# Attention with a window and block summaries, then a two-layer MLP: the first key load leads SyncE's queue, the first unit's probabilities are scaled while TensorE turns them, its means go by transfer, weights get a fourth staging place, and the order table is another

## The chip, the cores and the metric

The kernel runs on one core of a Trainium2 chip. The metric is the device time of a run in microseconds (us), lower is better. TensorE (PE) multiplies matrices, VectorE (DVE), ScalarE (ACT) and GpSimd (POOL) work on elements, SyncE (SP) issues nearly all transfers between the chip's memory (HBM) and the on-chip buffers.

## The reference

q, k and v are float32 with B=4, H=8, S=768, D=64; w_in is 512x2048 and w_out 2048x512, both with 64-bit elements in HBM. Cut to what is computed:

```python
k_sum = k.reshape(B, H, 24, 32, D).max(axis=3)
v_sum = v.reshape(B, H, 24, 32, D).mean(axis=3)
local = scale * q @ k.T          # kept where |pos_q - pos_k| < 16, else -1e9
blocks = scale * q @ k_sum.T + log(32)
a = softmax(concat([local, blocks], axis=-1))
attn = a @ concat([v, v_sum], axis=2)
x = attn.transpose(0, 2, 1, 3).reshape(3072, 512)
h = x @ w_in
out = (h - tanh(h)) @ w_out      # 3072x512, float32
```

## The kernel before, in words

**Units and pairs.** The 3072 rows of x are worked on in eight units of 384 rows (u = 0 to 7, two for each batch). A unit has four pairs of heads (p = 0 to 3). For a pair, TensorE turns keys and queries (`prep`), makes the scores (`scores`, into the PSUM tiles pS and pY), VectorE and ScalarE make the softmax (`softmax`, tile prob), the probabilities are turned (`transpose_probs`, tile probT) and multiplied by the values (`values`, tile vw, into pX or pY), and the result is split into a rounded part xh and a rest xl or vsum (`x_split`), so that products of parts have float32's precision. With the four pairs of a unit, the MLP runs over 16 slices f of w_in and w_out (`moe_in`, `moe_act_small`, `moe_split`, `moe_out`). For units 4 to 7 two units share products (`moe_pair`), and their x is kept in xf and other buffers. TensorE's work on all that is some 5,100 products.

**Softmax in unit 0.** For each of the six tiles of a pair (three row blocks of 128, two heads) VectorE makes mask and maximum and ScalarE an exponential with its sum; for each row block VectorE then makes the two sums and their inverses (stats<-stats), 12 times in the unit. Then `normal` scales the probabilities, 128x118 at a time, 24 times in the unit, on VectorE or ScalarE. `transpose_probs` turns them on TensorE by transposes against the identity. Unit 1 does the same; from unit 2 on, VectorE and transfers turn them.

**Means.** The first values (tile xh, 128x4x384) are halved by an addition (the task "pair", on VectorE or GpSimd), summed by TensorE against a block matrix (pX<-xh,vacc), read out by ScalarE (mean<-pX) and put behind the values of each of the six places in vw (24 rows). Unit 0 does that by four copies (`put_mean`, vw<-mean), the later ones by a transfer.

**Weights.** `convert(i)` (i even: slice i//2 of w_in, odd: of w_out) loads 128x512 elements of 64 bits into one of three staging places (tile raw, RAWB places), and makes float32 of them by four operations (a scaling tmp<-raw, a shift, the sign, a join), then a rounded part and a rest; the whole ones stay in tile wf for unit 0. A place is free again when the join has read it.

**Order.** What runs when is not decided at run time: `ORDER` is a table of task numbers, in which every engine takes its tasks, and `ELSEWHERE` says which engine takes a task that several could. `Plan.follow` goes through it with modelled costs, and where it foresees that TensorE would stand still before 100 us of its own clock, it puts in idle products of the identity with itself, pX<-ident (`keep_warm`); each shows as two records of 128x128. SyncE issues its transfers strictly in the table's order, with 8 in flight at most. Each engine waits by semaphores for what it reads. All instructions are issued through the helper class `Engine`, so every one has the same line, L233 (L235 after the change); the tiles tell them apart.

**End.** The last unit's y is copied out of PSUM by ScalarE (prob<-pS, prob<-pX, prob<-pT) and stored. A second program, for large h, follows behind a branch and is not taken.

Of the kernel before, what the change touches and what calls it, by code (L numbers as in the profile page):

```python
# [29 lines left out]
RAWB = 3  # L30
# [18 lines left out]
def phase(t):  # L49
# [486 lines left out]
def program(  # L536
# [210 lines left out]

    vd = v.rearrange("b h s d -> b s h d")


    def convert(i):
        f = i // 2
        tmp, res, place = ("wt", i), ("w", i), i % RAWB
# [826 lines left out]
```

## Time and profile before

| | |
|---|---|
| median of 3 runs | 641.96 us (640.52 to 648.61) |
| profiled execution | 641.7 us, its span 640.0 us |
| TensorE busy in the span | 624.0 us |
| VectorE, ScalarE, GpSimd busy | 486.6, 422.6, 172.5 us |
| granted clock of TensorE, mean | 0.995 |

The span goes from the first instruction to the end of the last; the time of a run has 1.7 us around it. A share of busy time is an average over the whole program. The views by stretch, the waits with what ended them, and the timelines of single engines tell in which part something can be gained or lost. "[1.41 <-DMA xl<-in_k_dram]" behind a row means that the engine had stood idle for 1.41 us and that this transfer released it.

### The profile page before, as it was taken

What the parts mean: (1) busy time and instruction counts of PE and PEld (TensorE: products, weight loads), DVE (VectorE), ACT (ScalarE), POOL (GpSimd) and SP (SyncE); (2) the same over time, 40 slices, a digit from 0 to 9 for tenths busy, and PEclk for the clock granted to TensorE, in tenths of its full rate; (3) what the DMA queues carried; (4) which work ended last, traced back from release to release, by engine and by line L of the source; (5) the groups of instructions that cost most, each with busy time, mean ns of one, the idle gap of its engine ahead of it and who ended that gap; (6) DMA issues with size and microseconds to landing.
All of it is one profiled execution on the core that took longest, in us unless ns stands there. A gap on an engine that the chain in (4) does not pass through costs nothing.

```text
span 640.0 us, 14660 instructions
## 1 busy us (share of the span) xinstructions
PE 624.0 (97%) x5163; PEld 532.0 (83%) x5163; DVE 486.6 (76%) x1349; ACT 422.6 (66%) x1270; POOL 172.5 (27%) x191
## 2 busy tenths in 40 slices
PE   6989999999999999999999999999999999999996
PEld 5877666688888888888888889988898889989995
DVE  3989999998797787567785788685659878677662
ACT  3979788678767777656767556555557754554545
POOL 2130003134313331130313104235351043315330
PEclk9989999999999999999999999999999999999998
DMA  8867886856687787877875641000000100000002
GB/s 297 199 197 225 226 231 191 182 116 185 162 165 161 186 228 167 186 174 160 236 198 165 192 132 55 0 2 1 0 2 1 65 35 1 1 1 1 2 0 102
DMA packets 159765, 77.27 MB, mean 121 GB/s; under 512 B 121704, under 2 KB 148552, under 8 KB 159688
## 3 DMA queue, kind: packets, MB, share of 16 engines
q1 hardware_dynamic: 159416, 76.09, 46.0%
q8 instruction: 42, 0.69, 0.5%
q14 instruction: 35, 0.29, 0.1%
q10 hardware_dynamic: 272, 0.20, 0.1%
HBM read 58.12 MB, written 17.84 MB: 119 GB/s over the span
## 4 chain that ended last, share of the span: by engine, by line
PE 85%; DVE 6%; DMA 4%; ACT 2%; SPq 1%; issue 1%; POOL 1%; DVEq 0%; POOLq 0%; ACTq 0%
PE pH L233 37%; PE pY L233 30%; PE pS L233 6%; PE pT L233 6%; PE pX L233 6%; DVE raw L233 2%; DMA raw<-in_moe_w_out_dram 1%; DVE tmp L233 1%; DVE prob L233 1%; SPq L233 1%; DMA xl<-in_k_dram 1%; DMA tmp<-in_v_dram 1%; DMA raw<-in_moe_w_in_dram 1%; DVE wf L233 1%; POOL xf L233 1%
## 5 line engine op out<-in xcount | busy, mean ns | idle before, releaser
L233 PE MATMUL pH<-xh,w 128*128 128x384 f32 x608 | 155.9, 346 | 0.0
L233 PE MATMUL pY<-wf,gh 128*128 128x512 f32 x321 | 133.9, 454 | 0.2 <-DVE gh L233 0.2
L233 ACT ACTIVATE prob<-prob,stats 128x118 f32<-128x118 f32 x298 | 109.4, 385 | 35.3 <-DVE stats L233 33.7
L233 PEld LDWEIGHTS pH<-xh,w 128*128 128x128 f32 x608 | 109.0, 188 | 9.2 <-issue 3.1
L233 POOL TENSOR_TENSOR gl<-gu,gh 128x384 fp32r<-128x384 f32 x45 | 46.9, 1041 | 134.1 <-ACT gh L233 71.7
L233 POOL TENSOR_TENSOR gu<-gu,gt 128x384 f32<-128x384 f32 x49 | 51.3, 1048 | 105.8 <-ACT gu L233 60.5
L233 PEld LDWEIGHTS pY<-wf,gh 128*128 128x128 f32 x321 | 59.4, 188 | 19.4 <-issue 10.8
L233 ACT ACTIVATE gu<-gu 128x384 f32<-128x384 f32 x128 | 65.7, 517 | 1.1
L233 ACT ACTIVATE gh<-gu 128x384 fp32r<-128x384 f32 x71 | 36.8, 520 | 42.3 <-PE pY L233 16.7
L233 PE MATMUL pH<-xl,w 128*128 128x384 f32 x192 | 64.6, 336 | 0.0
L233 ACT ACTIVATE gu<-tmp 128x384 f32<-128x384 f32 x64 | 33.2, 518 | 37.2 <-DVE gl L233 19.4
L233 DVE TENSOR_TENSOR gl<-gu,gh 128x384 fp32r<-128x384 f32 x67 | 41.1, 613 | 13.0 <-ACT gh L233 9.3
L233 DVE TENSOR_TENSOR gu<-gu,gt 128x384 f32<-128x384 f32 x63 | 35.5, 567 | 8.7 <-ACT gu L233 8.5
L233 ACT ACTIVATE gt<-pH 128x384 f32<-128x384 f32 x64 | 30.7, 482 | 15.8 <-PE pH L233 15.6
L233 ACT ACTIVATE gu<-pH 128x384 f32<-128x384 f32 x64 | 30.9, 482 | 14.3 <-PE pH L233 9.4
L233 ACT ACTIVATE gt<-tmp 128x384 f32<-128x384 f32 x64 | 32.4, 512 | 11.9 <-DVE tmp L233 7.9
L233 ACT ACTIVATION_READ_ACCUMULATOR prob<-prob,stats 128x1 f32 x192 | 36.6, 190 | 0.0
L233 PE MATMUL pY<-kT,gh 128*128 128x512 f32 x90 | 36.5, 406 | 0.0
L233 PEld LDWEIGHTS pH<-xl,w 128*128 128x128 f32 x192 | 36.0, 187 | 0.0
L233 PE MATMUL pY<-kT,gl 128*128 128x512 f32 x90 | 35.4, 394 | 0.0
L233 POOL TENSOR_TENSOR xf<-xf 128x256 f32<-128x256 f32 x25 | 19.5, 781 | 56.1 <-DVE xf L233 55.0
L233 DVE CUSTOM_DVE_ANT_0 prob<-pS,mask 128x118 f32<-128x118 f32 x96 | 25.6, 275 | 11.6 <-PE pT L233 10.2
(306 smaller groups left out, 1627.9 us busy)
## 6 DMA issues: line engine op xcount, KB each, us to landing
place<-turned SPq DMA_DIRECT2D x96, 96.0 KB
probT<-place SPq DMA_DIRECT2D x24, 384.0 KB
raw<-in_moe_w_in_dram SPq DMA_DIRECT2D x16, 512.0 KB
raw<-in_moe_w_out_dram SPq DMA_DIRECT2D x16, 512.0 KB
vw<-in_v_dram SPq DMA_DIRECT2D x80, 96.0 KB
rawq<-in_q_dram SPq DMA_DIRECT2D x96, 48.0 KB
tmp<-in_v_dram SPq DMA_DIRECT2D x24, 192.0 KB
raw<-in_k_dram SPq DMA_DIRECT2D x48, 96.0 KB
```

The lines of the kernel that those rows point to most:

```text
L233: return lambda *args, **kwargs: self._tc.keep_in_program_order(op(*args, **kwargs))
```

## The change

In unit 0 the inverse sums no longer scale the probabilities. They scale an identity (`diag`: `eye` times two inverse sums, 128x2x64, on VectorE, into the buffer of tile turned), and TensorE's turn is a plain product with that scaled identity where it was a transpose. `eye` is made once on GpSimd. The mean copies of unit 0 are gone; the transfer that the other units use takes their place. All loads of keys, queries, values and weights on SyncE are ordered behind the first key load. Weights get a fourth staging place in the buffer of xf, until units 4 and 5 need that for their x. The sums over chunks of values are trees of additions instead of reductions. The last slice (f = 15) of units 6 and 7 is worked on in three pieces of 128 columns, and one output copy is halved between ScalarE and VectorE. Three numbers of the planner's model are others, and ORDER and ELSEWHERE are other tables from end to end.

```diff
@@ the order, two of some 330 lines of tables
-    2, 6, 0, 1, 332, 9, 10, 7, 8, 13, 24, 220, 222, 224, 221, 226, 223, 252, 225, 254, 28, 35, 3, 14, 255, 227, 228, 230, 234, 232, 40, 258, 238, 236,
...
@@ planner
-    LARGE, TURN = 1.25, 0.9
+    LARGE, TURN = 9.0, 0.9
...
-        moved = nbytes / rate * (1.2 if kind == "w load" else 1.0)
+        moved = nbytes / rate * (1.12 if kind == "w load" else 1.0)
@@ program
+        first_home("xf", "xf", [P, 2 * DM + 64], U32)
+        eye = made["xf"][:, 2 * DM:].bitcast(F32)
...
+    do("const", POOL, 0.3, lambda: gpsimd.tensor_tensor(eye, ident[:, :64], ident[:, 64:], op=ALU.add), r=[IDENT], w=[EYE])
...
+    first_home(("dg",), "turned", [P, 2, 2 * NT, 64])
@@ convert
+    places = RAWB + small_only
...
-        tmp, res, place = ("wt", i), ("w", i), i % RAWB
+        tmp, res, place = ("wt", i), ("w", i), i % places
...
-            return raw[:, 2 * DM * place:2 * DM * (place + 1)]
+            return raw[:, 2 * DM * place:2 * DM * (place + 1)] if place < RAWB else made["xf"][:, :2 * DM]
@@ sum_chunks
-                vector.tensor_reduce(m[:, 1], x.rearrange("r t d -> r d t"), axis=AX.X, op=ALU.add)
+                x, m = at(st)[:96], at(acc)[:96]
+                for n in (4, 2, 1):
+                    to = m[:, 1] if n == 1 else x[:, :n * D]
+                    vector.tensor_tensor(to, x[:, :n * D], x[:, n * D:2 * n * D], op=ALU.add)
@@ put_mean
-        if u < 1:
-            for half in range(2):
-                either("mean copy", {DVE: 0.61, ACT: 0.86}, ...
-            return
@@ softmax
+            if u < 1:
+                i = x[0]
...
+                do("diag", DVE, 0.2, lambda i=i: vector.tensor_tensor(at(("dg", p))[:, 2 * i:2 * i + 2], eye.unsqueeze(1).broadcast_to([P, 2, 64]), at(st)[:, 3 * T + 2 * i:3 * T + 2 * i + 2].unsqueeze(2).broadcast_to([P, 2, 64]), op=ALU.mult), r=[EYE, (st, ("z", i))], w=[(("dg", p), i)])
+                continue
             for i in x:
                 for a in range(2):
                     either("normal", {DVE: 0.19, ACT: 0.3}, ...
@@ transpose_probs
-                        tensor.transpose(to[:, n, a], at(pr)[rows, n, a, :N2], ident[rows, rows])
+                        if u < 1:
+                            tensor.matmul(to[:, n, a], at(pr)[rows, n, a, :N2], at(("dg", p))[rows, 2 * n + a], start=True, stop=True)
+                        else:
+                            tensor.transpose(to[:, n, a], at(pr)[rows, n, a, :N2], ident[rows, rows])
@@ moe_act_small (as in moe_split and in moe_pair's last sum)
-        do("tanh", ACT, 0.37, lambda: scalar.activation(at(t), x(), AF.Tanh, scale=EC), r=[key], w=[(t, 0)])
+        for i, s in cuts(u, f):
+            n, c = seen_at(u, f, i), (s.stop - s.start - U) / 1400
+            do("tanh", ACT, 0.37 + c, lambda s=s: scalar.activation(at(t)[:, s], x()[:, s], AF.Tanh, scale=EC), r=[(key, i)], w=[(t, i)])
...
@@ store_y
+        if PAIRS and (u, i) == (PAIRED[2], NT - 1):
+            h = DM // 2
+            do("y out", ACT, 0.32, lambda: copy(scalar, at(ys)[:, :h], at(y)[:, :h], scale), r=[(y, 0)], w=[key])
+            do("y out", DVE, 0.33, lambda: copy(vector, at(ys)[:, h:], at(y)[:, h:], scale), r=[(y, 0)], w=[(ys, "half")])
...
@@ end of program
+    first = next(t for t in plan.tasks if t.kind == "k load")
+    for t in plan.tasks:
+        if t.kind in ("k load", "v load", "q load", "w load") and SP in t.costs and t is not first:
+            t.order.add(first)
```

The new functions are `cuts(u, f)`, three slices of 128 columns for the last slice of units 6 and 7 and one slice of 384 otherwise, and `seen_at`, the place of such a piece's sum.

SyncE's queue at the program's start. xl takes keys, xh values, rawq queries, vw values for the products, raw weights. Before:

```order
L233 DMA vw_125<-in_v_dram 16x4x64
L233 DMA rawq_96<-in_q_dram 128x2x192
L233 DMA xl<-in_k_dram 128x2x384 x2
L233 DMA xh<-in_v_dram 128x4x384 x2
L233 DMA raw<-in_moe_w_in_dram 128x4x256
L233 DMA raw<-in_moe_w_out_dram 128x1024
```

And now:

```order
L235 DMA xl<-in_k_dram 128x2x384
L235 DMA vw_131<-in_v_dram 16x4x64
L235 DMA rawq_97<-in_q_dram 128x2x192
L235 DMA xl<-in_k_dram 128x2x384
L235 DMA xh<-in_v_dram 128x4x384
L235 DMA raw<-in_moe_w_in_dram 128x4x256
L235 DMA xh<-in_v_dram 128x4x384
L235 DMA raw<-in_moe_w_in_dram 128x4x256
```

One key load stands ahead of the small value load and the query load, and a weight load stands ahead of the second values.

SyncE's queue some ten transfers later, around the first unit's values (vw). Before:

```order
L233 DMA vw_98<-in_v_dram 96x4x64 x4
L233 DMA rawq_271<-in_q_dram 128x2x192
L233 DMA raw<-in_moe_w_in_dram 128x4x256
L233 DMA xl<-in_k_dram 128x2x384
L233 DMA raw<-in_moe_w_out_dram 128x1024
```

And now:

```order
L235 DMA vw_99<-in_v_dram 96x4x64 x3
L235 DMA vw_99<-mean 24x6x256
L235 DMA vw_99<-in_v_dram 96x4x64
L235 DMA raw<-in_moe_w_in_dram 128x4x256
L235 DMA xl<-in_k_dram 128x2x384
L235 DMA vw_131<-in_v_dram 96x4x64
```

The transfer of the mean stands between the value loads, ahead of a weight load and the last key load.

TensorE from the second pair's scores to the turn of the first pair's probabilities (into pT and pY). Before:

```order
L233 MATMUL pS<-kT,q 64x94 x2
L233 MATMUL pY_282<-kT,q 64x94 x2
L233 MATMUL pX<-ident 128x128 x17
L233 MATMUL pT<-ident,prob 118x64
L233 MATMUL pY_368<-ident,prob 118x64
```

And now:

```order
L235 MATMUL pS<-kT,q 64x94 x2
L235 MATMUL pY_283<-kT,q 64x94 x2
L235 MATMUL pX<-ident 128x128 x9
L235 MATMUL pT<-turned,prob 118x64
L235 MATMUL pY_331<-turned,prob 118x64
```

Nine idle products stand where there were 17, and the turn reads turned, the scaled identity, instead of ident; in the whole first stretch they are 23 where there were 37.

## Rows read from the trace of the kernel before

**Rows 1.** The page's busy times: engine, us, share of the span, instructions.
```profile
PE 624.0 (97%) x5163; PEld 532.0 (83%) x5163; DVE 486.6 (76%) x1349; ACT 422.6 (66%) x1270; POOL 172.5 (27%) x191
```

**Rows 2.** Windows: us; busy (instructions) of PE, PEld, DVE, ACT, POOL; clock, DMA, GB/s.
```profile
46.40:128.00 81.60, 81.30 (x612) 55.70 (x611) 76.42 (x195) 67.72 (x180) 9.90 (x9) 1.00 0.80 212
13.00:42.00 29.00, 25.65 (x404) 21.08 (x405) 26.86 (x126) 24.81 (x83) 8.35 (x6) 0.95 0.85 221
40.00:44.00 4.00, 2.85 (x40) 2.38 (x39) 2.69 (x9) 2.66 (x5) 0.00 (x0) 0.67 0.75 225
```

**Rows 3.** Groups, TensorE to 46.4 us: busy us, mean ns, idle before, its releasers.
```profile
L233 PE MATMUL pX<-ident 128*128 128x128 f32 x74 | 12.3, 308 | 5.1 <-POOL ident L233 2.3 <-DVE vsum L233 1.5 <-ACT mean L233 1.2
```

**Rows 4.** Timeline of TensorE: start us, duration us, work, idle before it.
```profile
6.63 0.36 PE L233 MATMUL pH<-ident,xl 64*128 64x64 f32 x1 [1.41 <-DMA xl<-in_k_dram]
...
12.90 1.48 PE L233 MATMUL pX<-xh,vacc 128*24 128x256 f32 x6
...
16.23 0.24 PE L233 MATMUL pS<-top,q 64*64 64x24 f32 x2
...
17.23 4.06 PE L233 MATMUL pX<-ident 128*128 128x128 f32 x34
...
21.22 0.27 PE L233 MATMUL pT<-ident,prob 64*118 64x64 f32 x1
...
21.71 0.87 PE L233 MATMUL pH<-ident,rawq 128*128 128x128 f32 x6
...
24.01 0.92 PE L233 MATMUL pX<-probT,vw 118*64 118x64 f32 x24
...
37.72 0.24 PE L233 MATMUL pT<-ident,prob 64*118 64x64 f32 x1 [1.63 <-DVE prob L233]
```

**Rows 5.** Timelines of VectorE and GpSimd in the first 46 us.
```profile
10.32 0.96 DVE L233 TENSOR_TENSOR xh<-xh 128x768 f32<-128x768 f32 x1 [0.62 <-DMA xh<-in_v_dram]
...
12.45 1.81 POOL L233 TENSOR_TENSOR xh<-xh 128x768 f32<-128x768 f32 x1 [8.56 <-DMA xh<-in_v_dram]
...
17.36 0.07 DVE L233 MEMSET pS<- 64x15 f32 x1 [0.78 <-PE pY L233]
...
45.81 0.56 DVE L233 TENSOR_TENSOR vsum<-pY,xh 128x384 fp32r<-128x384 f32 x1 [0.73 <-ACT xh L233]
```

**Rows 6.** Tile mean: durations in ns (least/median/most), first and last start in us.
```profile
L233 DVE COPY vw<-mean x3: 679/680/1571, 15.6 to 32.6; 24x768 f32<-24x768 f32 x3
```

**Rows 7.** Groups, VectorE to 46.4 us; the xf row of the whole span.
```profile
L233 DVE TENSOR_SCALAR prob<-prob,stats 128x118 f32<-128x118 f32 x14 | 3.8, 297 | 0.0
L233 DVE SCALAR_TENSOR_TENSOR wf<-tmp,raw 128x512 uint32<-128x512 uint32 x3 | 2.0, 675 | 0.0
L233 DVE TENSOR_TENSOR vsum<-pX,xh 128x384 fp32r<-128x384 f32 x2 | 1.1, 552 | 0.0
L233 DVE TENSOR_SCALAR tmp<-raw 128x512 f32<-128x512 f32 x2 | 0.9, 426 | 0.0
...
L233 DVE TENSOR_TENSOR xf<-xf 128x256 f32<-128x256 f32 x39 | 17.6, 451 | 2.8 <-POOL xf L233 2.6
```

**Rows 8.** Groups, ScalarE to 46.4 us.
```profile
L233 ACT ACTIVATE prob<-prob,stats 128x118 f32<-128x118 f32 x34 | 12.4, 384 | 1.8 <-DVE stats L233 1.8
```

**Rows 9.** Waits, us/times/longest: TensorE behind 50 us, SyncE's queue to 130 us.
```profile
PE pH L233 <- DVE tmp L233: 1.0, 1, 1.0
PE pS L233 <- DVE rawq L233: 0.4, 1, 0.4
...
SPq L233 <- DVE raw L233: 23.9, 11, 3.2
```

**Rows 10.** Timeline of TensorE and ScalarE at the end.
```profile
633.86 0.39 PE L233 MATMUL pT<-vsum,gl 128*128 128x512 f32 x1
...
634.29 0.60 ACT L233 ACTIVATE prob<-pT 128x512 f32<-128x512 f32 x1
```

**Rows 11.** The chain of waits: a weight load in it.
```profile
80.80 5.02 DMA raw<-in_moe_w_out_dram
```

More of the change, by code (lines that the diff above doesn't have):

```diff
@@ L656, in program, with cuts, seen_at @@
     fixed(("mask",), [P, N2])
-    fixed(("sums_seen",), [P, NU * NF])
+    PAIRS = ((NU - 4, NU - 3), (NU - 2, NU - 1)) if small_only else ()
+    PAIRED = [u for pair in PAIRS for u in pair]
+    ENDS = [(u, NF - 1) for u in PAIRED[2:]]
+    fixed(("sums_seen",), [P, NU * NF + (NT - 1) * len(ENDS)])
+    def cuts(u, f):
+        return [(i, slice(P * i, P * i + P)) for i in range(NT)] if (u, f) in ENDS else [(0, slice(0, U))]
+    def seen_at(u, f, i):
+        return NU * NF + (NT - 1) * ENDS.index((u, f)) + i - 1 if i else NF * u + f
     sums_seen, SEEN = made[("sums_seen",)], ("sums_seen",)
@@ L660, in program @@
     fixed(("small",), [P, 1])
+    EYE = ("eye",), 0
+    if small_only:
+        first_home("xf", "xf", [P, 2 * DM + 64], U32)
+        eye = made["xf"][:, 2 * DM:].bitcast(F32)
+    else:
+        fixed(("eye",), [P, 64])
+        eye = made[("eye",)]
     unit, mask, ga, small = (made[n,] for n in ("ident", "mask", "ga", "small"))
@@ L889, in total @@
             def total(c=c, st=st):
-                x, m = at(st)[:96].rearrange("r (t d) -> r t d", d=D), at(acc)[:96]
-                vector.tensor_reduce(m[:, 1], x.rearrange("r t d -> r d t"), axis=AX.X, op=ALU.add)
+                x, m = at(st)[:96], at(acc)[:96]
+                for n in (4, 2, 1):
+                    to = m[:, 1] if n == 1 else x[:, :n * D]
+                    vector.tensor_tensor(to, x[:, :n * D], x[:, n * D:2 * n * D], op=ALU.add)
                 if c:
@@ L895, in total @@
                     vector.tensor_scalar(m[:, 0], m[:, 1], 1.0 / 32, None, op0=ALU.mult)
-            do("chunk sum", DVE, 1.25 if c else 1.1, total, w=[(st, 0), (acc, 0)])
+            do("chunk sum", DVE, 0.85, total, w=[(st, 0), (acc, 0)])
         place = buf(("means", b, g), "means", [NB, HG, D], F32, 2 * NG, scratch)
@@ L940, in put_mean @@
             dma("mean put", lambda e: e.dma_start(at(vw)[:NB].rearrange("r i f h d -> r (i f) (h d)"), at(place).rearrange("n h d -> n (h d)").unsqueeze(1).broadcast_to([NB, 2 * NT, HG * D])), 2 * NT * NB * HG * D * 4, 1024, r=[(place, 0)], w=[vw_keys(vw, i, half)[2] for i in range(NT) for half in range(2)])
-            return
-        if u < 1:
-            for half in range(2):
-                either("mean copy", {DVE: 0.61, ACT: 0.86}, lambda e, half=half: copy(e, at(vw)[:NB, :, half].rearrange("r i h d -> r i (h d)"), x.broadcast_to([NB, NT, HG * D])), r=[MEAN[g]], w=[vw_keys(vw, i, half)[2] for i in range(NT)])
             return
@@ L1057, in softmax @@
             do("inverse", DVE, 0.08, lambda n0=n0, n1=n1: vector.reciprocal(at(st)[:, 3 * T + n0:3 * T + n1], at(st)[:, 3 * T + n0:3 * T + n1]), w=[(st, ("z", x[0]))])
+            if u < 1:
+                i = x[0]
+                if i == 0:
+                    share(("dg", p), "dg", 2, lambda n: made[("dg",)][:, n])
+                do("diag", DVE, 0.2, lambda i=i: vector.tensor_tensor(at(("dg", p))[:, 2 * i:2 * i + 2], eye.unsqueeze(1).broadcast_to([P, 2, 64]), at(st)[:, 3 * T + 2 * i:3 * T + 2 * i + 2].unsqueeze(2).broadcast_to([P, 2, 64]), op=ALU.mult), r=[EYE, (st, ("z", i))], w=[(("dg", p), i)])
+                continue
             for i in x:
@@ L1068, in transpose_probs @@
             turned, place = ("tp", u, p), ("pd", u, p)
+            if (u, p) == (WHOLE, 0):
+                plan.waits[turned] = {t for n in range(NP) for t in plan.touch["dg", n]}
             buf(turned, "turned", [P, 4, 2 * NT, 32])
@@ L1081, in turn @@
                         rows, to = slice(64 * half, 64 * half + 64), at(ts[half])[:N2, :U].rearrange("p (n a r) -> p n a r", n=NT, a=2)
-                        tensor.transpose(to[:, n, a], at(pr)[rows, n, a, :N2], ident[rows, rows])
-        do("p turn", PE, 0.5, turn, r=[*r, IDENT], w=[(t, 0) for t in ts])
+                        if u < 1:
+                            tensor.matmul(to[:, n, a], at(pr)[rows, n, a, :N2], at(("dg", p))[rows, 2 * n + a], start=True, stop=True)
+                        else:
+                            tensor.transpose(to[:, n, a], at(pr)[rows, n, a, :N2], ident[rows, rows])
+        r += [(("dg", p), n) for n in range(NT)] if u < 1 else [IDENT]
+        do("p turn", PE, 0.5 if u else 0.9, turn, r=r, w=[(t, 0) for t in ts])
         for half, t in enumerate(ts):
@@ L1127, in x_split @@
            r=[(px, i) for i in range(NT)] + [(xh, p)], w=[(xl, p)])
-    PAIRS = ((NU - 4, NU - 3), (NU - 2, NU - 1)) if small_only else ()
-    PAIRED = [u for pair in PAIRS for u in pair]
     FIRST, HALF_F = NF * (NU - 4), NF // 2
@@ L1144, in x_keep @@
         spill = base not in (XF, XB)
+        if base == XF and n == 0:
+            plan.waits[base] = plan.users([(("raw",), n) for n in (2 * RAWB, 2 * RAWB + 1)] + [EYE])
         if n == 0:
@@ L1277, in add @@
         def add(to, x, ps):
-            do("h sum", DVE, 0.48, lambda: vector.tensor_tensor(part(to), part(x), at(ps)[:, :U], op=ALU.add), r=[(ps, 0)] + [x] * (to != x), w=[to])
+            for i, s in cuts(u, f) if to == h and n > 1 else cuts(0, 0):
+                do("h sum", DVE, dve(s.stop - s.start) + 0.015, lambda s=s: vector.tensor_tensor(part(to)[:, s], part(x)[:, s], at(ps)[:, s], op=ALU.add), r=[(ps, 0)] + [x] * (to != x), w=[(to[0], to[1] + i)])
         if n == 0:
@@ L1293, in moe_pair @@
             add(h, two, product(kk, "p4", w_half(2 * k + 1, 1), T4))
-        moe_act_small(u, f, h, lambda: part(h))
+        moe_act_small(u, f, h[0], lambda: part(h))
     def moe_in(u, f):
@@ L1314, in moe_act_small @@
         if key is None:
-            key, x = (("ph", u, f), 0), lambda: at(("ph", u, f))[:, :U]
+            key, x = ("ph", u, f), lambda: at(("ph", u, f))[:, :U]
         t, sq = (buf((n, u, f), n, [P, U], F32, 2) for n in ("gt", "gu"))
-        n = NF * u + f
-        do("tanh", ACT, 0.37, lambda: scalar.activation(at(t), x(), AF.Tanh, scale=EC), r=[key], w=[(t, 0)])
-        do("square", ACT, 0.478, lambda: scalar.activation(at(sq), x(), AF.Square, accum_out=sums_seen[:, n:n + 1]), r=[key], w=[(sq, 0), (SEEN, n)])
-        do("series", ACT, 0.42, lambda: scalar.activation(at(sq), at(sq), AF.Tanh, scale=EA), w=[(sq, 0)])
         g = g_base(u, f)
@@ L1323, in moe_act_small @@
             buf(g, g[0], [P, U], F32, 2)
-        either("g", {DVE: 0.469} if u == 0 else {POOL: 1.01, DVE: 0.469}, lambda e: e.tensor_tensor(at(g).bitcast(F32), at(sq), at(t), op=ALU.mult), r=[(sq, 0), (t, 0)], w=[(g, 0)])
+        for i, s in cuts(u, f):
+            n, c = seen_at(u, f, i), (s.stop - s.start - U) / 1400
+            do("tanh", ACT, 0.37 + c, lambda s=s: scalar.activation(at(t)[:, s], x()[:, s], AF.Tanh, scale=EC), r=[(key, i)], w=[(t, i)])
+            do("square", ACT, 0.478 + c, lambda s=s, n=n: scalar.activation(at(sq)[:, s], x()[:, s], AF.Square, accum_out=sums_seen[:, n:n + 1]), r=[(key, i)], w=[(sq, i), (SEEN, n)])
+            do("series", ACT, 0.42 + c, lambda s=s: scalar.activation(at(sq)[:, s], at(sq)[:, s], AF.Tanh, scale=EA), w=[(sq, i)])
+            c = (s.stop - s.start) / U
+            either("g", {DVE: 0.469} if u == 0 else {POOL: 0.14 + 0.87 * c, DVE: 0.065 + 0.404 * c}, lambda e, s=s: e.tensor_tensor(at(g)[:, s].bitcast(F32), at(sq)[:, s], at(t)[:, s], op=ALU.mult), r=[(sq, i), (t, i)], w=[(g, i)])
     def moe_act(u, f):
@@ L1359, in moe_split @@
         gh, gl = (buf((n, u, f), n, [P, U], F32R, RINGS[n]) for n in ("gh", "gl"))
-        either("g high", {ACT: 0.413, DVE: 0.269}, lambda e: copy(e, at(gh), at(w)), r=[(w, 0)], w=[(gh, 0)])
-        either("g low", {POOL: 1.01, DVE: 0.469}, lambda e: e.tensor_tensor(at(gl), at(w), at(gh).bitcast(F32), op=ALU.subtract), r=[(w, 0), (gh, 0)], w=[(gl, 0)])
+        for i, s in cuts(u, f):
+            c = (s.stop - s.start) / U
+            either("g high", {ACT: 0.413 + (c - 1) * 0.27, DVE: 0.069 + 0.2 * c}, lambda e, s=s: copy(e, at(gh)[:, s], at(w)[:, s]), r=[(w, i)], w=[(gh, i)])
+            either("g low", {POOL: 0.14 + 0.87 * c, DVE: 0.065 + 0.404 * c}, lambda e, s=s: e.tensor_tensor(at(gl)[:, s], at(w)[:, s], at(gh)[:, s].bitcast(F32), op=ALU.subtract), r=[(w, i), (gh, i)], w=[(gl, i)])
     outs = {}
@@ L1367, in moe_out @@
         whole = u == 0 and f in WHOLE_F
-        keys = [(g, 0), (("wf", w), 0)] if whole else [(("gh", u, f), 0), (("gl", u, f), 0), *w_keys(w)]
         n = outs[u] = outs.get(u, -1) + 1
@@ L1384, in go @@
                 tensor.matmul(at(y), gl, high, start=False, stop=last)
+            c = i if (u, f) in ENDS else 0
+            keys = [(g, 0), (("wf", w), 0)] if whole else [(("gh", u, f), c), (("gl", u, f), c), *w_keys(w)]
             do("out", PE, 0.86 if whole else 0.695, go, r=keys, w=[(y, 0)], before=[t for t in plan.tasks if t.kind == "seen turn" and i])
@@ L1400, in store_y @@
             key = ys, 0
-        do("y out", ACT, 0.5, lambda: copy(scalar, at(ys), at(y), 1.0 / (3.0 * EA * EC) if small_only else 1.0), r=[(y, 0)], w=[key])
+        scale = 1.0 / (3.0 * EA * EC) if small_only else 1.0
+        if PAIRS and (u, i) == (PAIRED[2], NT - 1):
+            h = DM // 2
+            do("y out", ACT, 0.32, lambda: copy(scalar, at(ys)[:, :h], at(y)[:, :h], scale), r=[(y, 0)], w=[key])
+            do("y out", DVE, 0.33, lambda: copy(vector, at(ys)[:, h:], at(y)[:, h:], scale), r=[(y, 0)], w=[(ys, "half")])
+            key = [key, (ys, "half")]
+        else:
+            do("y out", ACT, 0.5, lambda: copy(scalar, at(ys), at(y), scale), r=[(y, 0)], w=[key])
+            key = [key]
         r = u * U + P * i
-        dma("y store", lambda e: e.dma_start(out[r:r + P, :], at(ys)), P * DM * 4, 2048, r=[key])
+        dma("y store", lambda e: e.dma_start(out[r:r + P, :], at(ys)), P * DM * 4, 2048, r=key)
     def look():
         st, ps = share(("st", "seen"), "stats", 2, lambda n: made[("stats",)][:, n]), bank(("seen",), "pH")
-        do("seen", DVE, 0.2, lambda: vector.tensor_reduce(at(st)[:, 0:1], sums_seen, axis=AX.X, op=ALU.max), r=[(SEEN, n) for n in range(NM)], w=[(st, 0)])
+        do("seen", DVE, 0.2, lambda: vector.tensor_reduce(at(st)[:, 0:1], sums_seen, axis=AX.X, op=ALU.max), r=[(SEEN, n) for n in range(NM + (NT - 1) * len(ENDS))], w=[(st, 0)])
         do("seen turn", PE, 0.1, lambda: tensor.transpose(at(ps)[:1, :P], at(st)[:, 0:1], ident), r=[(st, 0), IDENT], w=[(ps, 0)])
@@ L1534, in program @@
                 sum_chunks(b, n // 2)
-    last_stores = set([t for t in plan.tasks if t.kind in ("y out", "y store")][-6:])
+    first = next(t for t in plan.tasks if t.kind == "k load")
+    for t in plan.tasks:
+        if t.kind in ("k load", "v load", "q load", "w load") and SP in t.costs and t is not first:
+            t.order.add(first)
+    last_stores = set([t for t in plan.tasks if t.kind in ("y out", "y store")][-(7 if PAIRS else 6):])
     def keep_warm():
```

317 rows, old and new, of tables (ELSEWHERE, ORDER) are left out of this document.

## The prediction

> **What bounds the kernel now.** I read the page first: TensorE is busy for 624.0 of 640.0 us [rows 1]. Then the same by stretches: from 46.4 to 128 us it is busy for 81.30 of 81.60 us [rows 2], and behind 50 us the table of waits has one stop of 1.0 us for it and one of 0.4 [rows 9]. So what can move lies before 46.4 us, in those stops, and in the tail. In the first stretch "busy" deceives. The order places 37 idle products of the identity with itself there to fill TensorE's gaps: 74 records, 12.3 us busy, with 5.1 us of stops in front of them, 2.3 of these the start [rows 3]. 34 of the records take 21.22 - 17.23 = 3.99 us, so one product, two records, costs 0.235 us [rows 4]. Two more stops, 1.41 for the first keys and 1.63 for probabilities, make 5.8 us without the start [rows 4].
>
> Who holds TensorE up there? From 13 to 42 us VectorE is busy for 26.86 of 29.00 us and ScalarE for 24.81 [rows 2]: the first unit's four softmaxes and the first weights share them. VectorE's last split of the first unit's x starts at 45.81 and takes 0.56 [rows 5]; from then on TensorE always has a product to do. So the question is when that split comes.
>
> **Start, up to the second pair's scores.** The first key load stands behind a small value load and a query load in SP's queue; TensorE waits 1.41 us for it, up to 6.63 [rows 4]. In the changed queue it stands first. The wait can shrink by 0 to 1.41; I take 1.3, since what stood ahead is about half its own size and more. That alone does not set the next step: TensorE takes the second pair's scores behind the sum over the first values, whose load has landed when VectorE's halving addition starts, at 10.32, with the same transfers ahead of it in both queues [rows 5]. That addition moves to GpSimd, where the other one took 1.81 us instead of 0.96 [rows 5]: 10.32 + 1.81 = 12.1, then six products, 1.48 us, and two fillers, 0.5: scores at about 14.1 instead of 16.23 [rows 4]. VectorE's first operation on them came 1.13 us later, at 17.36 [rows 5], and would come at 15.3. Gain **2.1 us**; bounds 0 (the value load later by what the keys gained, and GpSimd late) and 3.0 (no filler, the other waits gone).
>
> **VectorE and ScalarE, from there to the last split.** The order says what each has up to that split. VectorE loses 14 scalings of probabilities, 3.8 us busy, and gains 12 products of the identity with the inverse sums, 128x128 [rows 7]. No row shows that one; 128x384 takes 0.55 and 128x256 0.45, so 128 columns take about 0.35, and with the overlap of 0.03 that the scalings have, 12 of them 3.8: no gain (bounds: a gain of 1.4 at 0.2 each, a loss of 0.4 without the overlap). It loses two copies of the mean, 0.68 and 1.57: 2.25 [rows 6]. Of the weights one join (0.68), two scalings and a cast (0.43 each) now come behind the split, and one cast of x comes in (as much as the other cast): 1.5 [rows 7]. Together **3.7 us** less. ScalarE loses ten scalings at 12.4 / 34 = 0.36 [rows 8], 3.6, a cast of x and one of weights, some 1 us. Both engines are nearly full, so the smaller decides: 3.7; bounds 2.0 (gaps stay wherever a load or TensorE decides) and 5.0.
>
> One contention counts against it: the mean's copy took 1.57 us at its slowest, at 32.6, and 0.68 otherwise [rows 6], so something else on the chip stretches such an operation by 0.9 us; the halving addition that is new on GpSimd could do the same to VectorE once or twice. That is in the lower bound.
>
> **TensorE's turns.** The turn of a pair's probabilities is 12 + 12 transposes, 21.22 to 21.71, 0.49 us. As plain products with the scaled identity its nearest row is the 24 products with the values, also 64 columns each, 0.92 us [rows 4]. So +0.43 for each of four pairs, 1.7. Three of them lie beside the next pair's softmax, the last is on the path: **+0.4**; bounds 0.4 and 1.7. The Trainium skill says in "TensorE: Matmul & The Clock Gate" (Terms) that the transpose mode is four times faster for FP32. By that a turn would take 1.96 us and the sum would be 5.5 us higher; no run so far shows the operation itself.
>
> **Means by transfer.** The first unit's copies are in the sums above; two transfers take their place. SP stands at the first until ScalarE has the mean, which it makes right behind the sum over the values, now at 14 to 15 us; behind it in SP's queue wait a value load, a weight load, the last key load and the second half's values. A transfer that goes through a full queue takes up to 5.02 us [rows 11]: issued by 17 it is there by 22, and the products with the values, at 24.01 now [rows 4], would come at about 22. So 0; bounds 0 and 1.5. The last keys, which TensorE turns some 8 us later, have room.
>
> **At nothing.** The fourth staging place: SP's loads wait for VectorE to free one (23.9 us over 11 waits [rows 9]), but TensorE hardly waits for weights; were it to, the place would help. The tree sums: a reduction becomes additions of 256, 128 and 64 columns, 0.45, 0.35 and 0.30 by the rows above, about what a reduction takes; all lie under TensorE's products, and if that cover were gone they would cost their difference. The last units' pieces of 128 columns: TensorE has no stop in the last 100 us [rows 9], so nobody is released. The halved output copy is not the last one; the last starts 0.04 us after its product [rows 10], as it will.
>
> **Sum:** 641.7 (the profiled execution: span 640.0 and 1.7 around it) - 2.1 - 3.7 + 0.4 = 636.3. The median of the runs, 641.96, is 0.26 higher: 636.6, and I say **636.5**. A second way: the order has 23 fillers instead of 37, 14 x 0.235 = 3.3, less 1.7 for the turns: 1.6 if every stop that no filler covers stays, 7.4 if all 5.8 us of them go. The sum lies between.
>
> **The rivals.**
> A, the forecast: the head's gain reaches the end. 633.5 to 639.5. Chance 0.60.
> B, the gain is swallowed between 46 and 128 us. VectorE is busy for 76.42 of 81.60 us there [rows 2], with one more weight to convert now, and SP's loads hang on it. If TensorE, 5.4 us early, has to wait for weights, the end is where VectorE puts it: 640 to 642. For it: VectorE's 94%. Against it: VectorE also arrives 3.7 us earlier or more, and the loads have a place more. 0.20, at 641.
> C, a turn costs four times a transpose: 4 x 1.47 = 5.9, all on the path: 641.7 - 5.8 + 5.9 = 641.8. Against it: the products with the values, plain ones, at 0.92. 0.06.
> D, slower: the clock. TensorE stood still for 1.63 us up to 37.72 [rows 4], and the granted clock was 0.67 of full from 40 to 44, so half for a part of it [rows 2]. With 14 fillers fewer, a hole that the order does not foresee (the mean's transfer, late in front of the first pair's products with the values) is not filled; the clock falls, and the work behind the hole takes twice as long. About 20 us of products lie between the second scores and the end of the head; half of them at half clock cost 10: 641.7 - 5.4 + 10 = 646. It ends slower than before from 5.4 us of such products on. Against it: the holes shrink too. 0.06.
> E, more: all 5.8 us of stops in the head and the 1.4 behind it go together: 641.7 - 7.4 - 1.4 = 632.9. 0.08.
>
> **Range.** A, the middle of B, and the edge of E: 632.5 to 641.5, which leaves out some 0.2. Faster by over 2% (under 629.1) needs more than all the stops there are: 0.04. Slower by over 2% (over 654.8) needs D twice over: 0.03. Within 2%, about what a measurement of this kernel can tell from no change: 0.93.
>
> **What would show it.** The first key transpose at about 5.3 instead of 6.63; VectorE's first operation on the second scores near 15.3; the first unit's last split near 41 instead of 45.8; turns of 0.9 us (C: 1.96); 46 records of fillers; TensorE without stops from 41 on, and its last product near 629. B shows as TensorE's stops on weights between 41 and 128 us, D as a granted clock below 1 before 48. It is wrong altogether if the later order, new from end to end, has stops of its own behind 128 us: I put those at the present 1.4.

## The result, and the profile after

The changed kernel takes 646.32 us (median of 20 runs, 642.91 to 649.49), the kernel before 641.78 in the same runs: a ratio of 1.0067 (95% interval 1.0048 to 1.0086). It is slower by 4.5 us; 636.5 was forecast, 632.5 to 641.5 the range. The profiled execution took 648.91, span 647.2, so it lies 2.6 above its median and shows somewhat more of the loss than a usual run has.

The page's busy times, which answer to [rows 1]:

```profile
PE 628.3 (97%) x5183; PEld 533.0 (82%) x5183; DVE 489.6 (76%) x1415; ACT 414.4 (64%) x1257; POOL 180.8 (28%) x204
```

TensorE has 28 records of idle products fewer, and is busy for 4.3 us more. The windows, with columns as in [rows 2]:

```profile
46.40:128.00 81.60, 79.66 (x554) 53.34 (x552) 73.27 (x200) 66.25 (x173) 8.14 (x9) 1.00 0.75 197
120.00:130.00 10.00, 9.06 (x103) 6.99 (x101) 9.65 (x20) 5.93 (x15) 3.40 (x4) 1.00 0.67 130
130.00:140.00 10.00, 10.00 (x50) 7.68 (x44) 9.45 (x27) 4.22 (x15) 5.44 (x6) 1.00 0.70 118
140.00:150.00 10.00, 7.71 (x71) 6.01 (x71) 9.61 (x38) 7.18 (x24) 2.40 (x3) 0.83 0.43 115
```

And of the head, that is, the time up to the last split of the first unit's x:

```profile
20.00:30.00 10.00, 8.29 (x162) 7.33 (x162) 6.41 (x31) 6.82 (x21) 4.23 (x4) 0.88 0.92 258
30.00:40.00 10.00, 10.00 (x170) 7.75 (x168) 8.97 (x42) 8.72 (x28) 4.00 (x4) 0.95 0.89 201
```

TensorE, which stood for 0.3 us of the first stretch before, now stands for 1.9 there. From 120 to 150 us VectorE is busy for 95%; from 140 to 150 TensorE stands still for 2.3 us, and its granted clock is 0.83 there, that is, at its lower level, half, for a third of the time. 17% of 10 us is 1.7 us of work. The clock fell in the head too, to 0.88 and 0.95: another 1.7 us by the same sum. The kernel before has such a fall in its head as well [rows 2]. The waits of TensorE behind 50 us, as in [rows 9]:

```profile
PE pS L235 <- DVE top L235: 2.9, 2, 2.0
PE pH L235 <- ACT gu L235: 1.2, 1, 1.2
PE pH L235 <- DVE tmp L235: 0.8, 2, 0.6
PE pS L235 <- PE pH L235: 0.6, 1, 0.6
```

The list had 1.6 us in all, it has 7.2 now. Where the stops are, in the timeline of TensorE; the first two rows are places of the head that [rows 4] shows for the kernel before:

```profile
5.86 0.37 PE L235 MATMUL pH<-ident,xl 64*128 64x64 f32 x1
14.41 0.24 PE L235 MATMUL pS<-top,q 64*64 64x24 f32 x2 [0.44 <-DVE stats L235]
27.69 1.22 PE L235 MATMUL pX<-ident 128*128 128x128 f32 x4 [1.71 <-DVE vsum L235]
...
88.92 0.62 PE L235 MATMUL pH<-xh,w 128*128 128x384 f32 x2 [1.19 <-ACT gu L235]
128.87 0.30 PE L235 MATMUL pS<-top,rawq 64*64 64x24 f32 x4 [0.94 <-DVE top L235]
142.05 0.24 PE L235 MATMUL pS<-top,rawq 64*64 64x24 f32 x2 [1.99 <-DVE top L235]
253.04 0.30 PE L235 MATMUL pS<-top,rawq 64*64 64x24 f32 x4 [0.63 <-PE pH L235]
```

VectorE's last split of the first unit, at 45.81 in [rows 5], comes at 41.81:

```profile
41.81 0.56 DVE L235 TENSOR_TENSOR vsum<-pY,xh 128x384 fp32r<-128x384 f32 x1
```

So in these two traces the head gave 4.0 us, and more than twice that went later. How it went is seen when the work is counted: each product of TensorE at the median interval of its shape, idle products and turns left out, and the time read at which as much was done (worked out from all its records; e1, e9 and e10 are experiments below).

```
work done (us)   before   change     e1      e9      e10
   24             56.4     50.6     49.3    49.9    49.7
   60            108.5    105.7    102.5   102.9   103.0
   84            139.7    139.0    135.1   135.0   134.9
   96            153.5    157.7    152.0   151.0   149.3
  240            310.5    315.7    308.6   307.6   305.9
  552            628.7    634.9    627.9   626.8   625.1
span             640.0    647.2    640.1   639.0   636.8
```

The lead is 5.8 us at 50, 2.8 at 105, 0.7 at 139; behind 157 it is a lag of 4.2, at 315 of 5.2, at the end of 6.2. And the tail is 1.0 longer: from the start of the last product to the end, 647.2 - 640.04 = 7.2 us, 6.1 before [rows 10].

Not all of that belongs to the change. Up to 105 us e1 is the same program, and its trace is 3.2 us ahead there (102.5 against 105.7): in its head the clock did not fall, and it has no stop of 1.2 at 89. The execution shown lies 2.6 us above its median, e1's 0.4 below its own.

What makes VectorE late for `top`, the tile that TensorE waits for at 128.87 and 142.05? VectorE and GpSimd before the second of these stops:

```profile
134.70 1.27 DVE L235 TENSOR_TENSOR tmp<-tmp 96x256 f32<-96x256 f32 x2
136.00 0.51 DVE L235 TENSOR_TENSOR vacc<-tmp 96x64 f32<-96x64 f32 x1
136.55 0.92 DVE L235 TENSOR_SCALAR vacc<-vacc 96x64 f32<-96x64 f32 x1
137.39 1.86 DVE L235 TENSOR_TENSOR tmp<-tmp 96x256 f32<-96x256 f32 x2
...
140.96 0.94 DVE L235 TENSOR_REDUCE top<-raw 128x24 f32<-128x768 f32 x1
```

```profile
135.02 1.43 POOL L235 CAST vsum<-wf 128x512 fp32r<-128x512 f32 x2
136.41 1.01 POOL L235 TENSOR_TENSOR gl<-gu,gh 128x384 fp32r<-128x384 f32 x1
137.37 0.61 POOL L235 CAST vsum<-wf 128x512 fp32r<-128x512 f32 x1
137.94 1.17 POOL L235 TENSOR_TENSOR gu<-gu,gt 128x384 f32<-128x384 f32 x1
```

These are the tree sums. The two wider additions of one tree take 0.70 together elsewhere, 1.27 and 1.86 here, where GpSimd works without a gap; I call an operation stretched that takes longer than elsewhere. The operations by tile, with least, median and greatest ns, from 105 to 150 us:

```profile
L235 DVE TENSOR_TENSOR tmp<-tmp x24: 286/411/1499, 110.4 to 144.3; 96x256 f32<-96x256 f32 x12, 96x128 f32<-96x128 f32 x12
L235 DVE TENSOR_TENSOR vacc<-tmp x12: 220/222/516, 111.2 to 144.6; 96x64 f32<-96x64 f32 x12
```

Of the 72 additions in the whole trace 13 are stretched, up to four times, all of them beside work of GpSimd; two more that overlapped with such work are not. The reductions of the kernel before, in its trace:

```profile
L233 DVE TENSOR_REDUCE vacc<-tmp x24: 1032/1062/1086, 110.3 to 326.2; 96x64 f32<-96x512 f32 x24
```

None of the 24 was stretched, although GpSimd worked beside 15 of them. The Trainium skill has this in "SBUF — State Buffer" (Who interferes with whom): a VectorE operation with two inputs from SBUF contends with a GpSimd operation that reads SBUF, and a `tensor_reduce` never does on this chip. The trace agrees: 1.50 against 0.41 us for the one, 1.09 against 1.06 for the other. The planner's list of operations to be kept apart from GpSimd (HELD) does not have the chunk sums.

### The profile page after: what moved, and what is told of

It reads as the page before. It is cut to its first block, busy times and chain, and to the rows that moved or that the text cites. A ratio compares the mean times of both kernels' runs of the same rounds, so it can differ in the third digit from the quotient of the medians.

```text
span 647.2 us, 14756 instructions
## 1 busy us (share of the span) xinstructions
PE 628.3 (97%) x5183; PEld 533.0 (82%) x5183; DVE 489.6 (76%) x1415; ACT 414.4 (64%) x1257; POOL 180.8 (28%) x204
## 4 chain that ended last, share of the span: by engine, by line
PE 75%; DVE 11%; DMA 8%; ACT 2%; POOL 2%; issue 1%; SPq 0%; DVEq 0%; POOLq 0%; ACTq 0%
PE pH L235 31%; PE pY L235 27%; PE pS L235 6%; PE pT L235 6%; PE pX L235 5%; DMA raw<-in_moe_w_in_dram 2%; DVE tmp L235 2%; DMA xf<-in_moe_w_out_dram 1%; DVE prob L235 1%; DMA tmp<-in_v_dram 1%; DVE raw L235 1%; DMA raw<-in_moe_w_out_dram 1%; DVE xf L235 1%; DVE wf L235 1%; DMA xh<-in_v_dram 1%
## 5 line engine op out<-in xcount | busy, mean ns | idle before, releaser
L235 ACT ACTIVATE prob<-prob,stats 128x118 f32<-128x118 f32 x283 | 104.5, 386 | 44.4 <-DVE stats L235 42.5
L235 POOL TENSOR_TENSOR gl<-gu,gh 128x384 fp32r<-128x384 f32 (+1 forms) x49 | 49.8, 1018 | 161.7 <-ACT gh L235 93.0
L235 POOL TENSOR_TENSOR gu<-gu,gt 128x384 f32<-128x384 f32 (+1 forms) x50 | 50.6, 1014 | 99.8 <-ACT gu L235 66.6
L235 ACT ACTIVATE gu<-gu 128x384 f32<-128x384 f32 (+1 forms) x132 | 66.1, 507 | 1.3
L235 ACT ACTIVATE gh<-gu 128x384 fp32r<-128x384 f32 (+1 forms) x66 | 33.9, 515 | 46.1 <-PE pY L235 18.4
L235 ACT ACTIVATE gu<-tmp 128x384 f32<-128x384 f32 (+1 forms) x68 | 33.9, 498 | 38.0 <-DVE gl L235 22.0
L235 DVE TENSOR_TENSOR gl<-gu,gh 128x384 fp32r<-128x384 f32 (+1 forms) x67 | 40.4, 602 | 11.1 <-ACT gh L235 8.1
L235 DVE TENSOR_TENSOR gu<-gu,gt 128x384 f32<-128x384 f32 (+1 forms) x66 | 39.4, 600 | 3.8 <-ACT gu L235 3.6
L235 ACT ACTIVATE gt<-tmp 128x384 f32<-128x384 f32 (+1 forms) x68 | 32.9, 492 | 14.2 <-DVE tmp L235 12.0
L235 DVE CAST gh<-gu 128x384 fp32r<-128x384 f32 (+1 forms) x50 | 19.5, 391 | 14.9 <-PE pY L235 8.2
```

Source lines behind the costliest of these rows:

```text
L235: return lambda *args, **kwargs: self._tc.keep_in_program_order(op(*args, **kwargs))
```

## The experiments

Two theories at first. **GpSimd**: the tree's additions are stretched beside GpSimd's work, VectorE comes late, TensorE stops, and the clock falls. **Order**: VectorE is late at 128 to 145 us because the new order is too tight there, however it sums. Each ratio is to the kernel before on the same chip, with its 95% interval.

**e1**, reductions in the changed kernel:

```diff
-                x, m = at(st)[:96], at(acc)[:96]
-                for n in (4, 2, 1):
...
+                vector.tensor_reduce(m[:, 1], x.rearrange("r t d -> r d t"), axis=AX.X, op=ALU.add)
```

> The changed kernel with the chunk sums as one reduction again, as the kernel before has them; order and engines as in the change. Theory GpSimd: the two-operand additions of the tree are stretched two- to threefold while GpSimd works (0.29 to 1.50 us for tmp<-tmp), a reduction is not (1.03 to 1.09 in the kernel before); VectorE then has top in time, TensorE's stops of 0.94, 1.99 and 0.63 us on it and the stretch at a lower clock behind the second go: 646.3 - 3.6 - 1.5 = about 641.2, 640.5 to 642.5. Theory order: VectorE is late at 128 to 145 us because the new order gives it too much there, whichever way it sums; a reduction takes 1.06 where an undisturbed tree takes 0.95: 646 to 647, the stops stay.

642.37 us, 1.0010 (0.9989 to 1.0031): 4.0 less than the change, the intervals apart. So one piece of the change, the sums, holds nearly the whole loss against the kernel before. Of the stops on `top`, 0.3 us is left, but another has come. First all its reductions, then VectorE, then GpSimd and TensorE (start, busy time, then the wait in brackets):

```profile
L235 DVE TENSOR_REDUCE vacc<-tmp x24: 1001/1067/1097, 107.4 to 325.1; 96x64 f32<-96x512 f32 x24
```

```profile
141.14 2.62 DVE L235 TENSOR_SCALAR prob<-prob,stats 128x118 f32<-128x118 f32 x3
144.07 0.95 DVE L235 TENSOR_REDUCE top<-raw 128x24 f32<-128x768 f32 x1
```

```profile
141.13 1.02 POOL L235 TENSOR_TENSOR gl<-gu,gh 128x384 fp32r<-128x384 f32 x1 [6.08 <-ACT gh L235]
145.12 0.30 PE L235 MATMUL pS<-top,rawq 64*64 64x24 f32 x4 [1.15 <-issue]
```

Three scalings, 0.28 each elsewhere, take 2.62 beside GpSimd, though each reads one wide operand and not two, and the reduction that makes `top` stands behind them. The view puts TensorE's stop down to "issue"; that it waited for `top` is read from the times (the reduction ends at 145.02). Behind this shorter stop the clock did not fall:

```profile
140.00:150.00 10.00, 8.85 (x87) 7.54 (x86) 9.65 (x37) 7.64 (x29) 4.55 (x5) 1.00 0.59 164
```

**e2**, trees in the kernel before (the opposite edit).

> The kernel before with its 24 chunk sums as trees of additions; nothing else. Theory GpSimd: trees that fall beside GpSimd's work (at 110, 122, 135 to 138 and 143 to 148 us) are stretched by 0.5 to 1.5 us each, the others gain 0.1; TensorE, which has no stop there, gets some: 642.5 to 645.5. Theory order: the tree is as good as the reduction, 641.5 to 642.2.

642.83, 1.0023 (0.9998 to 1.0048): about 1 us slower, at the edge of what these runs tell. The additions are stretched there too (0.29 to 1.12 us), but TensorE hardly waits at those places: no stop over 0.5 is new. How much a stretch costs hangs on the slack that the order has there.

**e8**, the change with its trees, GpSimd quiet from 121 to 139 us (in ELSEWHERE):

```diff
+    214: 1, 767: 1, 813: 1, 815: 1,
-    783: 2, 785: 2, 795: 2, 799: 2, 803: 2, 805: 2,
```

> The changed kernel (646.3, trees of additions), and GpSimd's ten pieces of work between 121 and 139 us given to others: five copies to ScalarE, five two-operand operations to VectorE (0.55 to 0.7 each, so some 2.9 us more there). Theory GpSimd: with it quiet the trees take 0.95 each there (0.41, 0.29, 0.22 the additions), the stops of 0.94 and 1.99 us shrink although VectorE has more to do: 642 to 645. Rival (the trees are late for reasons of their own, VectorE is simply full): VectorE's 2.9 us more make it later: 647 to 649.

642.89, 1.0017 (0.9996 to 1.0037): 3.4 less than the change, with more work on VectorE. The trees there:

```profile
L209 DVE TENSOR_TENSOR tmp<-tmp x24: 286/334/425, 106.5 to 137.8; 96x256 f32<-96x256 f32 x12, 96x128 f32<-96x128 f32 x12
L209 DVE TENSOR_TENSOR vacc<-tmp x12: 220/221/223, 107.3 to 138.1; 96x64 f32<-96x64 f32 x12
```

Not one is stretched up to 138 us; of its later trees, beside GpSimd again, two are (additions of up to 1.24 us). With e1 that shows the cause: neither the tree nor GpSimd's work alone, but both at once. (I counted ten tasks, five copies; it was six copies and four others.)

**e10** and **e11**, light chunk sums in the changed kernel and in the one before, the question whether the head's gain is there at all:

```diff
+                vector.tensor_copy(m[:, 1], x[:, :D])
```

> The changed kernel with each chunk sum replaced by a copy of 64 columns (some 0.2 us instead of 1; the sums are left out of the result), so VectorE has 8 x 0.85 us less to do from 105 to 150. Theory: the head's gain of 5 to 6 us, there at 100 us, is given back at 120 to 150 because VectorE is full there (95% busy) and every stretched operation becomes a stop; with this room it reaches the end: 637.0 to 639.5. Rival: the gain is lost to the rest of the order, whatever VectorE has to do: 641.5 to 643.

> The kernel before with the same light chunk sums, left out of the result. It has no stop of TensorE between 100 and 300 us that a freer VectorE could take away, one of 0.4 at 320: 641.0 to 641.8 by both theories; more of a gain than 1.0 would say that the trace of the kernel before hides waits.

638.46, 0.9944 (0.9925 to 0.9963), and 641.15, 0.9993 (0.9972 to 1.0013). Less work on VectorE gives the changed kernel 7.9 us, 3.9 of them beyond e1, and the one before nothing. The lead of some 5 us goes through to 3.6 at the end in e10's column above; its tail, 6.6 us, takes 0.5 of it. Of what e10 is ahead of e1 at the end (2.8), 2.7 is there at 150 us. So the head's gain is real, and VectorE, full at 105 to 150 us, is where it is given back.

**e4** and **e9**, two tries to hand VectorE less. e4 is e1 with one rest of a weight (at 83.9 us) on VectorE instead of GpSimd; e9 is e1 with three scalings on ScalarE and the output copy whole.

```diff
+    154: 1,
...
+    675: 1, 676: 1, 679: 1,
```

> As the first of these (chunk sums by reduction), and the rest of one weight (w<-tmp,w, 1.29 us on GpSimd at 83.9) on VectorE, where it takes 0.69. Theory GpSimd: that work stretched VectorE's shift (xf<-xf, 0.43 to 1.63), by which ScalarE came late and TensorE stood for 1.19 us at 88.9; 1.0 us less than the first: 639.5 to 641.5. Theory order: VectorE has 0.69 us more to do and is later by that: 0 to 0.7 more than the first.

> The changed kernel with reductions, the output copy whole, and three scalings of probabilities (0.28 us each, 2.62 together beside GpSimd's work at 141 us) on ScalarE, which is busy for 3.6 of 5 us there. Theory GpSimd: VectorE has top 2 us sooner, TensorE's stop of 1.1 us at 144 goes: 640.5 to 641.3. Rival (the stop is handed on, as the rest of the weight was at 83.9): 641.8 to 642.3.

e4: 642.26, 1.0004 (0.9984 to 1.0024), no different from e1. It had little to take away: the stop of 1.19 us at 88.9 stands in the trace of the change, where VectorE's shift, late by a load, ran into that rest; in e1's trace the shift was done before it (0.42 us at 81.89), and no stop is there. The stop at 145, 1.15, stayed. e9: 641.02, 0.9991 (0.9973 to 1.0009). The stop at 145 is gone and nothing over 0.6 us is left behind 50 us, but it is no faster than the kernel before by what these runs can tell.

**e5**, e1 with the output copy whole.

> The changed kernel with reductions (642.37) and the halved output copy whole on ScalarE again. In the traces with the halved copy the last store's issue takes 2.3 us instead of 0.4 and 7.4 us lie from the start of the last product but one to the end, 6.4 in the kernel before. Theory: the halved copy costs that 1.0: 641.4, 640.9 to 641.9. Rival: the long issue comes from elsewhere (the stores' own queue, what is fetched at the end): 642.1 to 642.7.

642.02, 1.0014 (0.9994 to 1.0033): nearer to the rival. The last store's issue still takes 2.3 us, so the halved copy is not what makes it long. What stands beside it is an instruction fetch. DMA queues, first of the changed kernel from 639 us to its end, then of the kernel before from 633.9:

```profile
q14 instruction: 4, 0.03, 1.5%
q8 instruction: 1, 0.02, 1.5%
```

```profile
q14 instruction: 2, 0.02, 0.6%
```

Among the last three stores the changed kernel has a fetch of q8 (16 KB, 1.9 us) that the kernel before has ahead of them (1.1 us). In e4, e7 and e10 that fetch took 1.1 to 1.4 us, and the tail was 6.5 to 6.6 us instead of 7.1. No run takes the fetch away; that it costs the 1.0 us is open.

**e6**, e1 with the scalings on VectorE and the transposes back:

```diff
-                do("diag", DVE, 0.2, ...
+                do("diag", DVE, 0.38, lambda i=i: [normal(vector, i, a) for a in range(2)], ...
```

> The changed kernel with reductions (642.37), and the first unit's probabilities scaled on VectorE (24 scalings where 12 scaled identities were made, 0.28 us each, so 3.4 us more) and turned by transposes (4 x 0.86 us less on TensorE). Theory VectorE: it holds TensorE up in the head, the last split comes 1 to 3 us later than 41, and since VectorE and not TensorE decides to 145 us too, that reaches the end: 643 to 645. Rival TensorE: the plain products' 1.35 us are on the path, and the transposes give back what the scalings cost: 641.4 to 642.5.

644.02, 1.0052 (1.0029 to 1.0075): 1.7 more than e1, theory VectorE, with the intervals touching. By that, scaling on TensorE's side is worth having though its turn is dearer.

**e3**, transposes in the change, unscaled.

> The changed kernel with transposes against the identity in the first unit's turns; the scaled identities are still made and waited for, and the scaling by the inverse sums is left out of the result. Theory: a turn as a product takes 1.35 us in the changed kernel's trace and a transposing one 0.49, so TensorE has 4 x 0.86 = 3.4 us less to do before 40 us, of which 0.9 (the last turn) to 2 lie on the path; but what is gained in the head is eaten at 128 to 145 us by waits on VectorE, so the end moves by 0 to 0.5 only: 645.8 to 646.3. Rival: the head's time goes through to the end: 644.3 to 645.4.

Its time (1374 us) says nothing: unscaled probabilities make h large, and the second program runs. Only its head can be read, against that of the change (groups of TensorE to 46 us: busy, mean ns):

```profile
L235 PE MATMUL pT<-ident,prob 64*118 64x64 f32 x24 | 2.2, 226 | 0.0
```

```profile
L235 PE MATMUL pT<-turned,prob 64*118 64x64 f32 x48 | 6.0, 268 | 0.1
```

Turns cost 2.7 times as much busy time, yet e3's last split came at 43.18, no sooner than 41.81. That fits turns that lie beside the softmax; as heads of one program differ by 2 us (see the last section), a single trace shows no more than that. The end could not be tested this way.

**e7**, e1 with the first key load third again.

> The changed kernel with reductions (642.37), the first key load behind the small value load and the query load again. Theory: the first keys' turn comes 0.5 to 1.0 us later, the first scores too, but the second pair's scores wait for the value sums, whose load stands where it did; the end moves by 0 to 0.5: 642.4 to 642.9. Rival: the whole head moves with the first keys: 643.2 to 643.8.

643.31, 1.0033 (1.0012 to 1.0053): 0.9 more, nearer to the rival, though the intervals of e1 and e7 overlap. The second pair's scores came at 16.05 instead of 14.41: I had said that they wait for the value sums alone, and they don't; in both traces the stop in front of them is put down to VectorE's sums (stats).

**e12**, e1 with the means by ScalarE's copy.

> The changed kernel with reductions (642.37), the first unit's two transfers of the mean done by ScalarE as one copy each (24x1536, some 1.5 us by 0.83 for half of it). Theory (the transfer is hidden, the copy is on the path of a full ScalarE): 642.4 to 644. Rival (the transfer holds up SP's queue, so that the copy frees the loads behind it): 641 to 642.2.

642.31, 1.0005 (0.9986 to 1.0023): no difference from e1, neither theory's. The fourth staging place and the pieces at the end were not tried alone: without the place the order has to be another one.

## Why the prediction was wrong

**The step that failed first is "at nothing".** I priced the tree sums by undisturbed rows and said that they lie under TensorE's products. The first half is right (0.92 against 1.06), the second half is wrong. What decides is whether the operation can be stretched, and who is behind it on VectorE. The price: 646.32 - 642.37 = 4.0 us. In the trace it is the stops of 0.94 and 1.99 and the fallen clock behind the second; the one of 0.63 at 253 comes behind stretched additions too, is absent in e1 and 0.48 in e8, but the list puts it down to TensorE itself. I had a row for it, the mean's copy of 1.57 instead of 0.68 us [rows 6], expected GpSimd's addition to do such a thing in the head, and did not apply it to the sums.

**The second is A's condition, that the head's gain reaches the end.** Result and forecast lie 9.8 us apart. The sums are 4.0 of it. The 5.9 left are e1 against the forecast: e10 wins 3.9 of them by freeing VectorE, and its tail is 0.5 longer than before; some 1.5 stay open.

**The head (forecast 5.4 us, last split near 41): nearly right.** 41.81 in this trace, with a fallen clock in it, 39.8 to 41.1 in e1, e5, e8, e9 and e10. By this trace the 4.0 us are 1.2 up to VectorE's first operation on the second scores (2.1 forecast) and 2.8 from there (3.7 forecast). The first keys came at 5.86 (5.3 forecast; a query's turn stood ahead), the second scores at 14.41 (14.1). VectorE took those up at 16.16 (15.3), in part since a shift of 0.43 took 0.99 beside GpSimd's new halving addition: the contention that I had put into the bound.

**The turn: wrong size, no effect seen.** Forecast +0.43 each; it is 1.39 (35.10 to 36.49 us) against 0.49, +0.90. A pair's turn was 6 + 6 transposes with one record each, not the 12 + 12 that I wrote, and is 24 records now, as many as the products with the values that I took for its row (0.92). But of those, which have the form 118*64, two start every 0.06 us, of the turn's, with 64*118, two every 0.10; that the form is the reason was not tried. Rival C's price, 1.96, was as far off on the other side. Operation by operation it is 0.205 against 0.057 us, a factor of 3.6. The Trainium skill says in "TensorE: Matmul & The Clock Gate" (Terms) that the transpose mode is four times faster for FP32; the trace nearly agrees.

**Rival B (0.20) was what happened, and too mild.** VectorE takes the gain back, as e10 shows, but for the most part later than I placed it, up to 150 us and not at weights, and it did not end at 641: e1, at 642.4, is close to rival B. What pushed it beyond is the stretch. I gave B no price on the slow side, because I thought that a late VectorE can only cancel a lead; it can cost more, by the clock.

**Rival D's mechanism came, and small.** Its sign, a granted clock below 1 before 48, is there: in the head, from 27.5 to 31.0, at the end of the stop of 1.71 us, for 1.7 us and not 10; the kernel before lost as much there, and e1, e5, e8, e9 and e10 nothing, so it explains no loss against the kernel before. The second fall, from 143.6 to 147.0, is behind VectorE's late `top`.

**Means (0): right** as far as e12 can tell; the products with the values came at 22.68 (22 forecast). **First key (1.3): 0.9** by e7, though not clear of noise; its bearing on the second scores was wrong. **Tail (0): wrong** by 0.4 to 1.0 in the traces, cause open. **46 records of idle products: right**; the 1.4 us of stops behind 50: wrong, 7.2 us.

## What to carry to other kernels

When a VectorE operation is replaced, compare what its inputs are, not only its duration: in these traces additions of two operands from SBUF took up to four times as long beside GpSimd's work and a row of scalings three times, while no reduction took over 1.10 us instead of 1.06. A lead in the head is worth only as much as the next full engine lets through, so follow it to the stretch where a second engine is at 95%. A stop can cost more than its length: the one of 1.99 us here was followed by 3.4 us at half the clock. And read one trace with care: compare it with a run that is the same program up to the place in question.

## What was not expected of the hardware

Heads of the same code differ: the last split came from 39.8 to 41.8 us in six traces, so a single trace tells a head's gain to some 2 us only. The latest of them, that of the change, is the one of the six in which the clock fell in the head. And the position of an instruction fetch of 16 KB among the last stores goes along with a last issue of 1.6 to 2.3 us instead of 0.4 in every trace of the changed kernel that ends with these stores (e3 does not).
